# The Fourier step along the sequence, folded by a second symmetry (s and 384-s), with another order of the tokens

## The chip, the cores and the metric

The kernel runs on one core of a Trainium2 chip. The metric is the device time of one execution in microseconds (us). The profile comes from one execution taken by the hardware profiler; its span goes from the first to the last instruction. The engines are PE (TensorE, products), PEld (its weight loads), DVE (VectorE), ACT (ScalarE), POOL (GpSimd) and SP (SyncE, which issues most DMAs). SBUF is the on-chip memory of 128 partitions, PSUM the memory into which TensorE writes.

## The reference

There are two stages. First block-sparse attention for 4 batches and 8 heads, with 768 tokens and 64 features a head; then a Fourier mixing layer on the joined heads (768 x 512 per batch).

```python
scores = scale * np.matmul(q, k.transpose(0, 1, 3, 2))
scores = np.where(mask, scores, -1000000000.0)
attn = np.exp(scores - np.max(scores, axis=-1, keepdims=True))
attn = attn / (np.sum(attn, axis=-1, keepdims=True) + 1e-09)
x = np.matmul(attn, v)          # then (B, H, S, D) -> (B, S, H*D)

X = np.fft.fft(x, axis=1)       # along the sequence, S = 768
X = np.fft.fft(X, axis=2)       # along the features, 512
u = x + np.real(X)
un = (u - mean(u)) / np.sqrt(var(u) + 1e-06)
out = u + np.maximum(un @ w_ch1, 0.0) @ w_ch2     # 512 -> 2048 -> 512
```

Everything is computed in fp32.

## The kernel before, in words

**Tiles and the order of tokens.** The 768 tokens of a batch lie in six tiles of 128 rows. Tiles 0 to 2 form half 0 (`xA`), tiles 3 to 5 half 1 (`xB`), and row p of tile t in half 1 holds token (768 - s) mod 768 where row p of tile t in half 0 holds token s, apart from the ends. The order within the tiles is written out in `_ORDER`. An entry is (tile, first row, runs, jump, n, first token, step): `runs` runs of n rows each, the tokens of a run `step` apart, the runs `jump` apart. `_rows` turns an entry into DMA access patterns: with a positive jump one DMA with the dimensions [runs, n, columns], otherwise one DMA per run with [n, columns]. It serves the loads of the sine and cosine tables (`table_s`) and the stores of the output (`store`). `_TURNED` and `_IN_ORDER` are the same order as copies on ScalarE that place the columns of q: `turn` for the first five pairs of heads, `in_order` for the other eleven.

**Attention.** A pair of heads is 12 units; two units form a slot. For a slot TensorE makes the scores (`s`, L573), in some slots adds the mask by a product (L583), ScalarE takes the exponential (L593, L601), VectorE multiplies by the mask in later slots (L603), TensorE makes the values (`o`, L647), and sums are added up on GpSimd or VectorE (L633, L628). The result of a pair is transposed into x by `place` (L670 on TensorE, L671 on ScalarE) or by DMAs (`place_blocks`, L686).

**The Fourier step.** `fourier` computes the real part of the two transforms by symmetries: fold_0 makes sa = xA + xB and sd = xA - xB (s against 768-s), fold_1 and fold_2 fold the features twice, and fold_e makes `e1`, tile 1 of sa with another sign in row 0. `along(g)` multiplies along the sequence: for g = 0 and 1 the cosine part (`cosine`: two products over all 385 columns for tiles 0 and 2, then 192 and 193 columns for e1 and tile 1), for g = 2 and 3 the sine part (three products of 384 columns, L855); at g = 2 the 32 leftover columns go to `side` (L849). `keep_cosine` evacuates with three copies. `across(m)` then multiplies along the features, `arrive` adds to x, `spread` and `whiten` normalise.

**The channel layers.** `quad` makes a block of the first layer with seven products (L1045) and `channels` the second layer for one x tile (L1101, added to x at L1104). For batches 0 to 2 `channels` calls `store` for each tile after the last block; the last batch uses `outputs` (L1164) with stores in halves of the columns.

**The order of work.** The program is written out in order by a planner. It keeps an estimate of each engine's time (`when`) and of free PSUM banks, and takes the mixer's steps (`apart`, each with estimated costs) between the products of attention (`slot`) and of the channel layers of an earlier batch (`late`) where they seem ready (`gap`). Steps behind the folds wait until at most six channel steps are left. x has two buffers for each half, so batch b takes the buffer of batch b-2: `until` runs channel steps until the stores of that half are issued, and the first `place` of the new batch, whose copy is on ScalarE, writes into it.

Of the kernel before, what the change touches and what calls it, by code (L numbers as in the profile page):

```python
# [11 lines left out]
FP32 = mybir.dt.float32  # L12
# [5 lines left out]
ALU = mybir.AluOpType  # L18
# [22 lines left out]
def _grid(ap, start, runs, jump, n, step):  # L41
# [21 lines left out]
_TURNED = (((0, 64, 192, -64, 64, 1), (256, 64, 256, -192, 64, 1), (129, 63, 385, -384, 63, 1),  # L63
            (128, 127, 0, 384, 1, 1), (641, -128, 383, 127, 63, -1), (512, 127, 320, 191, 1, 1)),
           ((384, 64, 191, 64, 64, -1), (704, -128, 64, 63, 63, -1), (640, 127, 0, 1, 1, 1)))

_IN_ORDER = ((0, 129, (256, 127, 2), (64, -128, 2), (1, 2, 64)),  # L70
# [32 lines left out]
def kernel(  # L103
# [19 lines left out]
    P = 128  # L123
# [22 lines left out]
    cs_sb = const.tile([P, T, KS], FP32, name="cs_sb")  # L146
    sn_sb = const.tile([P, T, KS - 1], FP32, name="sn_sb")
# [5 lines left out]
    alt = const.tile([96, QD + 1], FP32, name="alt")  # L153
# [11 lines left out]
                            op0=ALU.mult)  # L165
    mask = const.tile([P, C, S], U8, name="mask")
# [212 lines left out]
    def table_s(src, dst, t):  # L379
        raw = tr_p.tile([P, ND * HS], FP32, tag="tr", name="tab")  # L380

        def get():
            for p0, cnt, rows in _rows(src, t):
                nc.sync.dma_start(out=raw[p0:p0 + cnt, 0:KS], in_=rows)

        def put():
            to = 0
            for runs, jump, n, s0, step in ODD_EVEN if dst is cs_sb else AS_PLACED:
                nc.vector.tensor_copy(
                    out=dst[:, t, to:to + runs * n].rearrange("p (r n) -> p r n", r=runs),  # L390
                    in_=_grid(raw, s0, runs, jump, n, step))
                to += runs * n
        return get, put

    AS_PLACED = [o[2:] for o in _ORDER if o[0] < T]
    ODD_EVEN = [AS_PLACED[i] for i in (0,)] + [(1, 0, 63, 259, 2), AS_PLACED[3], AS_PLACED[1],
                                               (1, 0, 63, 2, 2), AS_PLACED[4], (1, 0, 1, 384, 1)]

    def table_d(src, dst):
# [7 lines left out]
        def put():  # L407
            if dst is cd_sb:
                nc.vector.memset(alt, 0.0)
                for to, frm in ((dst, raw), *((alt[g:g + 1, :], row) for g in (0, 32, 64))):  # L410
                    nc.vector.tensor_copy(out=to[:, 0:QD + 1], in_=frm[:, 0:KD:2])
                nc.vector.tensor_copy(out=dst[:, QD + 1:KD], in_=raw[:, 1:KD:2])
            else:
# [6 lines left out]
                   for t in range(T)]  # L420
# [70 lines left out]
    def turn(n, a, half):  # L491
# [19 lines left out]
        else:  # L511
            for i, (to, to_jump, frm, jump, cnt, step) in enumerate(_TURNED[half]):
                on, copy = (("DVE", nc.vector.tensor_copy) if n == 0 and half == 1
                            else ("ACT", nc.scalar.copy))
                copy(out=_grid(dst, to, 2, to_jump, cnt, 1),
                     in_=_grid(tp, frm, 2, jump, cnt, step))
                end = busy(on, 0.27 if cnt > 1 else 0.18, done)
# [250 lines left out]
    def fourier(b, xA, xB, uns):  # L768
# [17 lines left out]
        def fold_e():  # L786

            sa, _, e1 = st["f"]
            b1 = xB[:, 1, :]
# [3 lines left out]
                                           in1=sa[:, 1, 0:M + 1], op0=ALU.mult, op1=ALU.add)  # L793

        def fold_2(i):
# [3 lines left out]
            if i != 1:  # L799
# [9 lines left out]
        folds = [lambda: fold_0(0), lambda: fold_0(1), lambda: fold_1(0), fold_e,  # L809
                 lambda: fold_1(1), lambda: fold_2(0), lambda: fold_2(2), lambda: fold_2(1)]  # L810

        parts = slice(DM - QD, DM), slice(0, QD)

        def along(g):
# [7 lines left out]
            odd = S // 4  # L822

            def cosine(ps, rows, cols):
                mm = nc.tensor.matmul
                for t in (0, 2):
                    mm(ps[rows, 0:KS], sa[:, t, cols], cs_sb[:, t, :], start=(t == 0), stop=False)  # L827
                mm(ps[rows, 0:odd], e1[:, cols], cs_sb[:, 1, 0:odd], start=False, stop=False)
                mm(ps[rows, odd:KS], sa[:, 1, cols], cs_sb[:, 1, odd:KS], start=False, stop=True)

            def keep_cosine(dst, ps):
                nc.scalar.copy(out=dst, in_=ps[:, 0:KS])

                nc.scalar.copy(out=_grid(dst, P + 1, 2, 63, 63, 1),
                               in_=_grid(ps, P, 2, 65, 63, 1))
                nc.scalar.copy(out=_run(dst, P, 2, P - 1), in_=_run(ps, P + 64, 2, -1))

            if g < 2:
                cosine(ps, slice(0, P), parts[g])
                keep_cosine(st["zc"][:, g, :], ps)  # L840
                return
            if g == 2:
                side, at = ps_t.tile([P, 512], FP32, tag="t", name="side"), bank("t")
                for i, (lhs, t, cols) in enumerate(((sa[:, 0, :], 0, slice(0, KS)),
                                                    (sa[:, 2, :], 2, slice(0, KS)),
                                                    (e1, 1, slice(0, odd)),
# [772 lines left out]
```

## Time and profile before

| | us |
|---|---|
| time, median of 3 runs | 1061.93 (1061.48 to 1063.14) |
| span of the profiled execution | 1059.7 |
| mean of one 128x385 record (L827) / 128x192 (L828) / 128x384 (L855) | 0.493 / 0.324 / 0.497 |
| all records of L827, L828, L829, L855, L849 together, busy | 11.9 + 3.9 + 3.9 + 17.3 + 5.5 |
| VectorE, scalar_tensor_tensor over 257 elements (L792), each | 0.488 |
| ScalarE, evacuations of the cosine part (L832, L834, L836), each | 0.481, 0.264, 0.162 |

A line of a group has the line of the kernel, the engine, the operation, output and inputs, shapes, the number of records, then busy time and mean of one, then the idle time ahead of them. A matmul's record reaches to its modelled end and overlaps the next one's, so the time that a product occupies TensorE is read from the distance of the starts. An fp32 product makes two records. In the DMA rows, the digit is the mean share of 16 DMA engines in tenths, and the row of GB/s is what they moved in each of 40 equal slices.

### The profile page before, as it was taken

How to read it: one execution, taken by the hardware profiler on the slowest of the kernel's cores; microseconds unless marked ns; L12 is line 12 of the kernel's file. 1: busy time of each engine (PE TensorE's matmuls, PEld its weight loads, DVE VectorE, ACT ScalarE, POOL GpSimd, SP SyncE). 2: the span in 40 equal slices, each digit the busy share in tenths (PEclk: the TensorE clock that was granted, in tenths of full speed). 3: DMA queues.
4: the chain of work that ended last, by engine and by line, in shares of the span. 5: the costliest groups of instructions: out<-in, count | busy, mean ns of one | idle time of the engine just before them, and what ended most of it. 6: DMA issues, size and time to landing. Idle time of an engine off the chain costs nothing.

```text
span 1059.7 us, 12422 instructions
## 1 busy us (share of the span) xinstructions
PE 1036.7 (98%) x4390; PEld 535.8 (51%) x4390; DVE 654.7 (62%) x1218; ACT 374.3 (35%) x742; POOL 235.6 (22%) x262
## 2 busy tenths in 40 slices
PE   8999999999999999999999999999999999999996
PEld 4333345444455554444444555444445554578575
DVE  6898894667645445664668364765457455575663
ACT  6978855664030112342441302253220211210210
POOL 1000183537000002454553001256520001000000
PEclk9999999999999999999999999999999999999998
DMA  7757422220000002212220001221000001000001
GB/s 214 231 168 232 117 46 45 45 47 15 1 0 1 1 0 48 59 29 54 42 54 2 1 0 30 60 38 28 11 11 6 1 0 32 29 0 1 1 20 43
DMA packets 120803, 46.65 MB, mean 44 GB/s; under 512 B 108176, under 2 KB 113822, under 8 KB 120734
## 3 DMA queue, kind: packets, MB, share of 16 engines
q1 hardware_dynamic: 119484, 45.06, 17.3%
q10 hardware_dynamic: 1218, 0.72, 0.3%
q8 instruction: 36, 0.59, 0.2%
q14 instruction: 33, 0.27, 0.1%
q0 software_dynamic: 32, 0.01, 0.0%
HBM read 37.11 MB, written 6.29 MB: 41 GB/s over the span
## 4 chain that ended last, share of the span: by engine, by line
PE 89%; DVE 4%; DMA 3%; ACT 2%; issue 1%; SPq 0%; POOL 0%; ACTq 0%; DVEq 0%
PE y L1101 23%; PE z L1045 15%; PE s L573 12%; PE o L647 10%; PE yp L1045 7%; PE yy L1164 7%; PE xp L1045 4%; PE zp L855 2%; DMA out_dram<-x 1%; PE s L583 1%; PE zp L827 1%; PE sp L714 1%; PE sp L728 1%; PE utp L970 1%; PE xt L670 1%
## 5 line engine op out<-in xcount | busy, mean ns | idle before, releaser
L633 POOL TENSOR_TENSOR acc<-acc,e 128x384 f32<-128x384 f32 x158 | 159.3, 1042 | 94.1 <-DVE e L603 75.1
L573 PE MATMUL s<-qT,kT 64*128 64x384 f32 x768 | 154.0, 516 | 7.7 <-ACT e L593 4.3
L647 PE MATMUL o<-e,vr 128*64 128x384 f32 x768 | 141.8, 497 | 0.0
L1101 PE MATMUL y<-w_sb,hB 128*128 128x512 f32 x288 | 128.2, 596 | 1.0 <-DVE x L1104 1.0
L1101 PE MATMUL y<-w_sb,hA 128*128 128x512 f32 x288 | 128.4, 595 | 0.0
L603 DVE TENSOR_TENSOR e<-s,mask 128x768 f32<-128x768 f32 x92 | 83.8, 951 | 57.6 <-ACT s L601 47.8
L1104 DVE TENSOR_TENSOR x<-y,x 128x512 f32<-128x512 f32 x72 | 49.7, 690 | 110.9 <-PE y L1101 110.8
L573 PEld LDWEIGHTS s<-qT,kT 64*128 64x128 f32 x768 | 64.2, 186 | 85.8 <-issue 22.1
L601 ACT ACTIVATE s<-s 128x768 f32<-128x768 f32 x92 | 69.9, 792 | 87.5 <-PE s L573 87.0
L1045 PE MATMUL z<-unT,t 128*128 128x384 f32 x256 | 93.1, 486 | 1.2 <-DVE hA L1050 1.2
L633 POOL TENSOR_TENSOR acc<-e 128x384 f32<-128x384 f32 x42 | 47.1, 1142 | 211.6 <-ACT e L593 126.7
L1050 DVE TENSOR_TENSOR hA<-z,hA 128x384 f32<-128x384 f32 x64 | 35.7, 557 | 87.5 <-PE z L1045 87.5
L593 ACT ACTIVATE e<-s 128x768 f32<-128x768 f32 x100 | 76.1, 815 | 36.2 <-PE s L583 31.2
L1101 PEld LDWEIGHTS y<-w_sb,hB 128*128 128x128 f32 x288 | 53.4, 190 | 67.7 <-issue 65.0
L918 POOL TENSOR_SCALAR st<-st 128x1 f32<-128x1 f32 x24 | 8.6, 358 | 346.9 <-DVE st L917 346.8
L1101 PEld LDWEIGHTS y<-w_sb,hA 128*128 128x128 f32 x288 | 53.3, 190 | 62.8 <-issue 59.7
L647 PEld LDWEIGHTS o<-e,vr 128*64 128x64 f32 x768 | 47.9, 136 | 70.3 <-issue 67.9
L1054 ACT ACTIVATE hA<-hA 128x384 f32<-128x384 f32 x64 | 33.5, 523 | 120.3 <-DVE hA L1050 119.9
L1045 PEld LDWEIGHTS z<-unT,t 128*128 128x128 f32 x256 | 48.5, 190 | 35.5 <-DVE hA L1050 2.1
L1054 ACT ACTIVATE hB<-hB 128x384 f32<-128x384 f32 x64 | 33.5, 523 | 86.5 <-DVE hB L1050 84.2
L1065 ACT COPY hA<-xp 128x384 f32<-128x384 f32 x32 | 15.3, 478 | 97.9 <-PE xp L1045 97.9
L1045 PE MATMUL xp<-unT,w_sb 128*128 128x384 f32 x128 | 47.2, 492 | 0.0
(202 smaller groups left out, 1428.7 us busy)
## 6 DMA issues: line engine op xcount, KB each, us to landing
wraw<-in_moe_w_ch_dram SPq DMA_DIRECT2D x32, 512.0 KB
vr<-in_v_dram SPq DMA_DIRECT2D x30, 192.0 KB
qb<-in_q_dram SPq DMA_DIRECT2D x44, 96.0 KB
kb<-in_k_dram SPq DMA_DIRECT2D x44, 96.0 KB
x<-oT SPq DMA_DIRECT2D x192, 12.0 KB
out_dram<-x SPq DMA_DIRECT2D x15, 128.0 KB
out_dram<-x SPq DMA_DIRECT2D x7, 256.0 KB
qr<-in_q_dram SPq DMA_DIRECT2D x24, 64.0 KB
```

Source lines behind the costliest of these rows:

```text
L573: nc.tensor.matmul(s[:, i, 0:HS], kT[rows, c * P:(c + 1) * P], qT[rows, queries], start=True, stop=u not in by_pe)
L593: nc.scalar.activation(out=e, in_=s[:, :, 0:HS], func=ACT.Exp, scale=scale)
L601: nc.scalar.activation(out=s[:, :, 0:HS], in_=s[:, :, 0:HS], func=ACT.Exp, scale=scale)
L603: nc.vector.tensor_tensor(out=e, in0=s[:, :, 0:HS], in1=m.broadcast_to([P, 2, HS]), op=ALU.mult)
L633: nc.gpsimd.tensor_add(out=acc[:, i, :], in0=start[:, i, :], in1=e[:, i, :])
L647: nc.tensor.matmul(o[D * i:D * i + D, :], vt[:, i, c, :], e[:, i, :], start=(c == 0), stop=(c == C - 1))
L1045: nc.tensor.matmul(to, a[:, k, :], c[:, k, :], start=(k == 0), stop=(k == ND // 2 - 1))
L1050: tt(out=to, in0=ps, in1=a, op=ALU.add)
L1054: nc.scalar.activation(out=h, in_=h, func=ACT.Relu)
L1101: nc.tensor.matmul(y, hs[0, half][:, l, m * P:(m + 1) * P], w2_sb[:, 4 * r + l, :], start=(l == 0), stop=(l == 3))
L1104: nc.vector.tensor_tensor(out=x[:, m, :], in0=y, in1=x[:, m, :], op=ALU.add)
L1164: nc.tensor.matmul(ps, a[:, k, :], c[k // 2][:, k % 2, :] if isinstance(c, list) else c[:, k, :], start=(k == 0), stop=(k == 3))
```

## The change

The token order now pairs s with 384-s as well: tiles 0 and 1 of half 0 hold the tokens 0 to 255, tile 2 the tokens 384-s for tile 0 (with 256, 257 at its ends), and half 1 the mirrored ones. With this a second fold (`fold_s`, six VectorE operations per batch) makes from tiles 0 and 2 one tile for the odd and one for the even frequencies. Each frequency column then needs two products instead of three, and the table tiles for t = 2 are gone. The columns of the tables are placed in the order odd, even (`FREQUENCIES`), the evacuation (`keep`) restores an order with whole tiles, the frequency 384 and token 0 now lie in m = 0 instead of m = 1, and the planner's lists and estimated costs follow. `_TURNED` and `_IN_ORDER` become lists of copies with up to three dimensions, and the lists of two runs in `_ORDER` have a jump of 1.

```diff
-_ORDER = ((0, 0, 2, -128, 64, 129, 2),
-          (1, 0, 1, 0, 1, 0, 1), (1, 1, 2, -257, 63, 259, 2), (1, 127, 1, 0, 1, 257, 1),
-          (2, 0, 2, -128, 64, 256, 2),
-          (3, 0, 2, 128, 64, 639, -2),
-          (4, 0, 1, 0, 1, 384, 1), (4, 1, 2, 257, 63, 509, -2), (4, 127, 1, 0, 1, 511, 1),
-          (5, 0, 2, 128, 64, 512, -2))
+_ORDER = ((0, 0, 2, 1, 64, 0, 2), (1, 0, 2, 1, 64, 128, 2),
+          (2, 0, 1, 0, 1, 256, 1), (2, 1, 2, 1, 63, 382, -2), (2, 127, 1, 0, 1, 257, 1),
+          (3, 0, 1, 0, 1, 384, 1), (3, 1, 2, 1, 63, 766, -2), (3, 127, 1, 0, 1, 641, 1),
+          (4, 0, 1, 0, 1, 640, 1), (4, 1, 2, 1, 63, 638, -2), (4, 127, 1, 0, 1, 513, 1),
+          (5, 0, 1, 0, 1, 512, 1), (5, 1, 1, 0, 63, 386, 2), (5, 64, 1, 0, 64, 385, 2))
...
-    cs_sb = const.tile([P, T, KS], FP32, name="cs_sb")
-    sn_sb = const.tile([P, T, KS - 1], FP32, name="sn_sb")
+    cs_sb = const.tile([P, 2, KS], FP32, name="cs_sb")
+    sn_sb = const.tile([P, 2, KS - 1], FP32, name="sn_sb")
...
+    first_row = ident[:, 0:1]
+    not_first = const.tile([P, 2], FP32, name="not_first")
...
+        def fold_s(i):
+
+            def plus(out, tile, by, to):
+                nc.vector.scalar_tensor_tensor(out=out[:, 0:M + 1], in0=tile[:, 0:M + 1], scalar=by,
+                                               in1=to[:, 0:M + 1], op0=ALU.mult, op1=ALU.add)
+
+            sa, sd, e1 = st["f"]
+            if i == 0:
+                plus(e1, sa[:, 2, :], not_first[:, 1:2], e1)
+                plus(sa[:, 0, :], sa[:, 2, :], not_first[:, 0:1], sa[:, 0, :])
+                plus(sa[:, 1, :], sa[:, 2, :], first_row, sa[:, 1, :])
+                plus(sa[:, 2, :], sa[:, 2, :], flip, sa[:, 1, :])
+            else:
+                plus(sd[:, 0, :], sd[:, 0, :], not_first[:, 0:1], sd[:, 2, :])
+                plus(sd[:, 2, :], sd[:, 2, :], -2.0, sd[:, 0, :])
...
-            def cosine(ps, rows, cols):
-                mm = nc.tensor.matmul
-                for t in (0, 2):
-                    mm(ps[rows, 0:KS], sa[:, t, cols], cs_sb[:, t, :], start=(t == 0), stop=False)
-                mm(ps[rows, 0:odd], e1[:, cols], cs_sb[:, 1, 0:odd], start=False, stop=False)
-                mm(ps[rows, odd:KS], sa[:, 1, cols], cs_sb[:, 1, odd:KS], start=False, stop=True)
...
+            def keep(dst, ps, n):
+                nc.scalar.copy(out=_at(dst, 64, [(-64, 2), (P, T), (1, 64)]),
+                               in_=_at(ps, 0, [(ODD, 2), (64, T), (1, 64)]))
+                if n == KS:
+                    nc.scalar.copy(out=dst[:, n - 1:n], in_=ps[:, n - 1:n])
+
+            def product(to, table, *terms):
+                ps, ks = to
+                for t, lhs in enumerate(terms):
+                    nc.tensor.matmul(ps, lhs, table[:, t, ks], start=(t == 0), stop=(t == 1))
...
-                cosine(ps, slice(0, P), parts[g])
-                keep_cosine(st["zc"][:, g, :], ps)
+                cols = parts[g]
+                product(odd(ps, slice(0, P)), cs_sb, e1[:, cols], sa[:, 2, cols])
+                product(even(ps, slice(0, P), ODD + 1), cs_sb, sa[:, 0, cols], sa[:, 1, cols])
+                keep(st["zc"][:, g, :], ps, KS)
...
-            for t in range(T):
-                nc.tensor.matmul(ps[:, 0:KS - 1], sd[:, t, parts[g - 2]], sn_sb[:, t, :],
-                                 start=(t == 0), stop=(t == T - 1))
-            nc.scalar.copy(out=zs[:, g - 2, 0:KS - 1], in_=ps[:, 0:KS - 1])
+            cols = parts[g - 2]
+            product(odd(ps, slice(0, P)), sn_sb, sd[:, 0, cols], sd[:, 1, cols])
+            product(even(ps, slice(0, P)), sn_sb, sd[:, 2, cols], sd[:, 1, cols])
+            keep(zs[:, g - 2, :], ps, KS - 1)
...
-                 d(1.0, fold_1, 1), d(1.2, fold_2, 0), d(0.6, fold_2, 2), d(1.3, fold_2, 1)]
-        first += [("mt" if g == 2 else "m", lambda g=g: along(g), 2.1, (1.0 if g < 2 else 0.5), 0.0)
+                 d(1.0, fold_1, 1), d(1.8, fold_s, 0), d(1.2, fold_2, 0), d(0.6, fold_2, 2),
+                 d(0.9, fold_s, 1), d(1.3, fold_2, 1)]
+        first += [("mt" if g == 2 else "m", lambda g=g: along(g), (2.1 if g == 2 else 1.4), 0.5, 0.0)
```

More of the change, by code (lines that the diff above doesn't have):

```diff
@@ L419 @@
     table_steps = [(table_s, (src, dst, t)) for src, dst in ((cos_s, cs_sb), (sin_s, sn_sb))
-                   for t in range(T)]
+                   for t in range(2)]
     table_steps += [(table_d, (cos_d, cd_sb)), (table_d, (sin_d, sd_sb))]
@@ L896, in arrive @@
             x = (xA, xB)[half][:, m, :]
-            if m == 1 and half == 1:
+            if m == 0 and half == 1:
                 row = st["zs"][0:1, 0, :]
```

102 lines of the change are left out of this document (49 added, 53 removed), and 10 rows, old and new, of tables (_IN_ORDER, _TURNED).

## The prediction

> **What bounds the kernel now.** I read the page first: span, busy times, the slices and the chain of waits.
>
> ```profile
> span 1059.7 us, 12422 instructions
> PE 1036.7 (98%) x4390; PEld 535.8 (51%) x4390; DVE 654.7 (62%) x1218; ACT 374.3 (35%) x742; POOL 235.6 (22%) x262
> PE   8999999999999999999999999999999999999996
> ...
> PE 89%; DVE 4%; DMA 3%; ACT 2%; issue 1%; SPq 0%; POOL 0%; ACTq 0%; DVEq 0%
> ```
>
> TensorE is the bound nearly everywhere: busy 98%, 89% of the chain. A product taken away shortens the run if nothing else makes TensorE stand. The three medians lie 2.2 us above this span (1061.93 against 1059.70); I build the sum on the span and add 2.2 at the end.
>
> Next, the timeline of TensorE where batch 2 is transformed; start, length, engine, line, tile. Ends are modelled, so I take differences of starts.
>
> ```profile
> 583.64 1.46 PE L827 MATMUL zp<-cs_sb,sa 128*128 128x385 f32 x4
> 584.94 0.49 PE L828 MATMUL zp<-cs_sb,e 128*128 128x192 f32 x2
> 585.26 0.49 PE L829 MATMUL zp<-cs_sb,sa 128*128 128x193 f32 x2
> 585.59 1.45 PE L1045 MATMUL yp<-t,w_sb 128*128 128x384 f32 x4
> ...
> 597.48 2.20 PE L855 MATMUL zp<-sn_sb,sd 128*128 128x384 f32 x6
> 599.52 1.45 PE L1045 MATMUL yp<-t,w_sb 128*128 128x384 f32 x4
> ```
>
> Each fp32 product is two records. One over 385 columns takes (584.94-583.64)/2 = 0.65 us, one over 192 takes 0.32, so the time goes with the columns, down to half the width.
>
> The third view is the stores of x, by their DMA traffic: first the three x tiles of half 0 of batch 2, then the three of half 1.
>
> ```profile
> GB/s 0 0 0 0 0 0 116 212 191 225 130 0 0 0 0 0 0 7 0 150 184 130 198 178 27 0 0 0 0 0 0 0 198 212 219 205 41 0 0 0
> ...
> GB/s 0 0 25 16 49 20 29 45 20 57 49 49 49 57 49 49 49 41 37 37 45 49 53 49 53 49 49 53 49 53 49 53 49 70 49 53 33 0 0 0
> q1 hardware_dynamic: 392, 0.79, 11.2%
> ```
>
> The first row covers 885 to 897 us (0.3 us a slice): each tile is gone in some 1.5 us at about 200 GB/s. The second covers 898 to 918 (0.5 us a slice): the same 0.79 MB needs 17.5 us at 49 GB/s, and 11.2% of 16 engines over 20 us is 36 engine-us, so two engines work. The two halves differ in how `_rows` describes the rows. Tiles 0 to 2 are issued as single runs of 63 or 64 rows (their jump is negative, so the runs are split). Tiles 3 to 5 have a positive jump: one DMA whose outermost dimension is the two runs. Two runs, two engines.
>
> Last, what a late store costs: the stage in which batch 2's x takes over the buffer of batch 0.
>
> ```profile
> 408.64 0.49 PE L670 MATMUL xt<-ident,oT 128*128 128x128 f32 x3
> ...
> 412.25 0.48 ACT L671 COPY x<-xt 128x384 f32<-128x384 f32 x1 [2.82 <-PE o L647]
> 412.63 1.51 ACT L601 ACTIVATE s<-s 128x768 f32<-128x768 f32 x2
> 413.47 1.82 DVE L603 TENSOR_TENSOR e<-s,mask 128x768 f32<-128x768 f32 x2 [4.37 <-ACT s L601]
> ...
> 414.48 1.78 PE L573 MATMUL s<-qT,kT 64*128 64x384 f32 x8 [1.12 <-DVE e L603]
> ```
>
> The copy into x (L671) has its input by 409.1 but starts at 412.25. The `o` named is not an input; what it must wait for is the last of the three stores of that buffer, issued at 409.6. Behind it on ScalarE stand the exps, behind them VectorE's masks, behind them TensorE's scores, which stood 1.12 us. So this chain already reaches TensorE.
>
> **The change, part by part.**
>
> *Products along the sequence.* Per batch, two cosine groups go from two 385-column products plus 192 and 193 (1.95 us, 583.64 to 585.59) to four of 192 or 193 (4 x 0.325 = 1.30): 2 x 0.65 = 1.30 less. Two sine groups go from three of 384 (2.04 us, the second 1.93) to four of 192 (1.30): 1.26 less after a switch of some 0.1. The side products, which run beside each other in groups of 32 columns, take about 0.7 us either way. 2.56 x 4 batches = **-10.2 us** (bounds -10.9 to -9.6). This step stands on rows of the very same shapes.
>
> *VectorE and ScalarE.* fold_s adds six SCALAR_TENSOR_TENSOR over 257 elements per batch; L792, the same form, takes 0.49 us with 0.40 from start to start: 24 x 0.40 = 9.6 us in all. In batches 0 to 2 they lie under products (TensorE is busy 12.00 of 12 us from 300 to 312). In batch 3 the folds end at 814.6 and the first product along the sequence follows at 817.6; 2.4 us more uses that slack up, and a missed gap moves it to 822. Its last whitening ends at 872 and the first transposes that are held for the last six channel steps come at 878.4, so 4.5 us still fits. If it didn't, it would cost up to that much. I take **+0.5** (0 to +4.5). The evacuations lose two small copies for each cosine group. The reordering of q on ScalarE goes from six copies (2 x 0.43, 2 x 0.31, 2 x 0.20) to seven, 0.2 us more in 11 pairs on an engine that is 35% busy: nothing.
>
> *Start and tables.* Two tables fewer are loaded and copied (18 small copies of 0.14 to 0.22 us, two waits of SP's queue for a free buffer). Against it, four of the remaining loads get two runs, hence two engines: 128 rows of 1.5 KB, some 4 us each at 49 GB/s, in the stretch in which weight loads once kept ScalarE waiting 3.3 us. The mask's query spread gets 4 more casts of 0.11 us, twice, and VectorE two setup instructions; off_q is ready at 8.0 us and first used at 9.0. I take **+0.5** (-2 to +2).
>
> *Stores of x.* This is a part that the words of the change do not name. All two-run entries of the new `_ORDER` have jump +1: tiles 0 and 1 become one two-run DMA each, tile 2 two single rows and a two-run DMA, tiles 3 and 4 likewise; only tile 5 is single runs (1, 63 and 64 rows). So the slow form moves from half 1 to the whole of half 0 and two tiles of half 1: 1.30 MB per batch on two engines where it was 0.78.
>
> Where half 0 is reused, the price can be worked out. For batch 2 the stores start at 401.38, 405.25 and 409.13; first bytes come 1.05 us after an issue (885.75 to 886.8). 0.782 MB at 49 GB/s is 16.0 us, so the last byte leaves at 418.4; at the 42 GB/s that half 1 had here (421.8 to 440.3) it is 420.9. I take 419.0, because VectorE and GpSimd stand still meanwhile, plus 0.4 to the copy (440.2 to 440.65 in half 1): 419.4 instead of 412.25. Nothing else is queued on TensorE ahead of those scores: **+7.2** (+5 to +9). For batch 3 the stores start at 651.78: last byte 652.8 + 16.6 = 669.4, copy at 669.9, first masks 0.4 + 0.85 us later, scores 1.0 after that, 672.1 instead of 668.17: **+4.0** (0, if the planner puts another channel step ahead of the copy, to +6). Half 1 gains: its copy waited 1.86 us for the last store at 440.65 and TensorE stood 0.74; with tile 5 spread that goes: **-0.7** (-0.7 to 0).
>
> *The end.* Before, the last packet (1057.1) belongs to tile 5 of half 1, on two engines. Now tile 4 and tile 1 (0.25 MB each) are followed on the same two engines by the two halves of tile 2's rows (0.13 MB, 2.6 us each), the second issued after 1051.4: from 1039 with 252 KB at the slow 14 to 24 packets per us seen there to 1046.4, 256 KB to 1051.7, then 2.9, 1.0 for tile 5's share and 2.9, so 1058.5: **+1.4** (-1 to +2.2).
>
> The Trainium skill (DMA: Bandwidth & Descriptors, section Why a DMA increments its semaphore by 16 and not by 1) says that a DMA runs on the largest number of engines up to 16 that divides the slowest dimension of both access patterns, whatever its steps; for the new entries that is two engines again, which makes the first rival below less likely than the rows alone do.
>
> Sum: -10.2 + 0.5 + 0.5 + 7.2 + 4.0 - 0.7 + 1.4 = +2.7. 1059.7 + 2.7 + 2.2 = **1064.6 us**: slower, though TensorE has less to do.
>
> **The rivals.**
> 1. The stores don't stay on two engines: every two-run store in the trace has a row step of -2, the new tiles 0 and 1 have +2 and a jump of one row. If they spread, all waits stay as they are: 1061.9 - 10.2 + 0.8 = 1052.5, faster. For it: no two-run row with a positive step exists. Against: single runs of either step spread. 0.12.
> 2. The two waits are half covered, as the planner lays a channel step (3.4 us) ahead of each copy, as it did in batch 3 (659.55 to 663.1): 1064.6 - 2 x 2.1 = 1060.4. Against: for batch 2 there was none. 0.20.
> 3. VectorE's folds miss gaps in the last batch (+4.5) or the table loads delay the weights (+2): about 1069. 0.13.
> 4. The forecast, 1064.6, with a range of its own of 1060.5 to 1068. 0.55.
>
> **Chances.** A measurement here tells some 0.2% (2.1 us) from no change: 1059.8 to 1064.1 is the same. The forecast puts 0.43 above and 0.12 within; rival 1 all below; rival 2 0.06 below and 0.14 within; rival 3 all above. That is 0.18 faster, 0.26 same, 0.56 slower. The range, 1056 to 1069.5, leaves rival 1 and a tail of rival 3 out.
>
> **What would show it.** Records of 192 columns at 0.32 us a product and no 384 ones in `zp`; six more instructions of the form of L792 per batch; DMA at 49 GB/s for some 16 us after half 0's last stores; the copy into x some 7 us later after its transposes than before for batch 2, and the scores behind it; for half 1 no wait. Wrong if half 0's stores run at 200 GB/s, if TensorE's busy time falls by much less than 10 us, or if stalls appear at the folds.

## The result and the profile after

The changed kernel takes **1099.54 us** (median of 4 runs, 1098.12 to 1099.61) against 1062.08 us before (4 runs, 1061.48 to 1063.14): a ratio of **1.0349, 95% interval 1.0335 to 1.0364**, 37.5 us slower. The forecast was slower by 2.7. The direction was right, the size was not: 1099.5 lies far outside the range of 1056 to 1069.5.

The page of the changed kernel: the span, busy time of each engine, TensorE's busy tenths, the granted clock in tenths, and the head of the chain of waits, by engine.

```profile
span 1097.8 us, 12462 instructions
PE 1043.4 (95%) x4414; PEld 542.8 (49%) x4414; DVE 666.8 (61%) x1231; ACT 366.9 (33%) x736; POOL 230.7 (21%) x258
...
PE   8969999998999998999999998978999999999995
...
PEclk9989999999999998999999999999999999999998
...
PE 81%; DVE 5%; SPq 4%; DMA 4%; ACT 3%; issue 1%; POOL 0%; DVEq 0%; ACTq 0%; POOLq 0%
```

TensorE stands in places where it did not: at slices 3, 10, 16, 25 and above all 27 and 28 of 40. Outside its busy time there were 23.0 us before (1059.7 - 1036.7); now there are 54.4 (1097.8 - 1043.4). And its busy time, which should have fallen by 10, rose by 6.7: part of it runs at a lower granted clock, as the row PEclk shows at two of these places (the kernel's mean is 0.984, before 0.995).

The saving itself is there. Timeline of TensorE in batch 2, the first cosine group along the sequence (start, length, line, tile):

```profile
608.54 0.49 PE L854 MATMUL zp<-cs_sb,e 128*128 128x192 f32 x2
608.87 1.14 PE L854 MATMUL zp<-cs_sb,sa 128*128 128x192 f32 x6
609.85 1.45 PE L1064 MATMUL yp<-t,w_sb 128*128 128x384 f32 x4
```

From 608.54 to 609.85 is 1.31 us for four products; the forecast was 1.30, before it was 1.95.

The first place that the forecast had not seen, SP's queue from 59 us (L387 loads a table, L389 the one row that replaces row 0 of the sine table, L261 is q, L454 the weights; an `x6` is six issues in a row):

```profile
59.09 0.55 SPq L387 DMA_DIRECT2D tab<-in_sin_s_dram  x1
65.42 0.27 SPq L389 DMA_DIRECT2D tab<-in_sin_s_dram  x1
65.81 3.85 SPq L261 DMA_DIRECT2D qr<-in_q_dram  x6
69.71 1.55 SPq L454 DMA_DIRECT2D wraw<-in_moe_w_ch_dram  x3
```

The row lands in the same partition as row 0 of the load ahead of it, so its issue waits until that load has landed: SP does nothing from 59.64 to 65.42. The view of SP's waits (what waited for what: us in total, times, longest) says the same:

```profile
SPq L389 <- DMA tab<-in_sin_s_dram: 5.7, 1, 5.7
```

Behind it stand six loads of q and the weights. What that does on TensorE (in brackets the idle time before, and what ended it):

```profile
67.47 0.85 PE L717 MATMUL sp<-e,pick 128*32 128x384 f32 x8
76.84 2.93 PE L576 MATMUL s<-qT,kT 64*128 64x384 f32 x8 [8.52 <-ACT e L596]
```

ScalarE waited 9.41 us for the weights' chunk (its L463 at 74.89), the exps stand behind that, and TensorE stood 8.52 us. The scores after it take 2.93 us where eight records of them otherwise take 1.56. The kernel before has a shorter stop at this place, and the scores behind it are slow too; its granted clock is 0.57 from 70 to 74 us:

```profile
70.01 2.46 PE L573 MATMUL s<-qT,kT 64*128 64x384 f32 x8 [2.40 <-ACT e L593]
```

The second place was forecast, the copy of batch 2's x into the buffer of batch 0. ScalarE, and TensorE beside it:

```profile
422.68 0.59 ACT L990 COPY unT<-utp 128x512 f32<-128x512 f32 x1 [3.90 <-PE utp L989]
429.25 0.48 ACT L674 COPY x<-xt 128x384 f32<-128x384 f32 x1 [5.98 <-DMA out_dram<-x]
```

```profile
422.48 0.49 PE L673 MATMUL xt<-ident,oT 128*128 128x128 f32 x3
...
431.47 2.93 PE L576 MATMUL s<-qT,kT 64*128 64x384 f32 x8 [4.28 <-DVE e L606]
```

Its input is there by 423.0, the copy waits for the store of the old x until 429.25; again the scores behind the stop take 2.93 us. The same happens for batch 3: the copy starts at 684.50, the scores at 686.73 after 4.46 us of idle time.

The third place is the largest: the attention of the last batch. Work in windows of 20 us (busy time and instructions of PE, PEld, DVE, ACT, POOL, then the granted clock, DMA share, GB/s), after and then before:

```profile
710.00:730.00 20.00, 16.19 (x92) 6.23 (x92) 12.75 (x15) 10.94 (x22) 17.31 (x19) 1.00 0.23 37
730.00:750.00 20.00, 15.47 (x80) 5.60 (x80) 13.07 (x15) 8.53 (x12) 14.20 (x15) 0.91 0.16 35
750.00:770.00 20.00, 16.23 (x78) 5.77 (x75) 11.36 (x16) 5.09 (x7) 16.34 (x17) 0.91 0.12 18
```

```profile
710.00:730.00 20.00, 20.00 (x91) 8.11 (x88) 11.31 (x15) 8.92 (x17) 11.58 (x12) 1.00 0.20 41
730.00:750.00 20.00, 20.00 (x81) 7.95 (x79) 9.34 (x12) 5.43 (x8) 7.69 (x8) 1.00 0.07 11
```

Before, TensorE was full there: channel products of batch 2 ran between the scores. After, there are none in this stretch; batch 2's first `y<-w_sb,hA` (record 192 of that tile) starts at 788.28 instead of 716.24 (before, then after):

```profile
716.24 1.98 PE L1101 MATMUL y<-w_sb,hA 128*128 128x512 f32 x4
...
788.28 4.03 PE L1120 MATMUL y<-w_sb,hA 128*128 128x512 f32 x9
```

Attention alone leaves TensorE waiting 12.1 us in these three windows: 5.8 for VectorE's masks (L606), 5.1 for its output transposes (L658), the rest for sums. The transposes themselves wait there, 9.8 us in all, for the DMA that carries an earlier block out of the same buffer (`x<-oT`).

At the end, TensorE's last product ends at 1086.04 and the span 11.7 us later; before it was 8.8 us.

### The profile page after: what moved, and what is told of

Its sections match the earlier page's. It is cut to its first block, busy times and chain, and to the rows that moved or that the text cites. A ratio compares the mean times of both kernels' runs of the same rounds, so it can differ in the third digit from the quotient of the medians.

```text
span 1097.8 us, 12462 instructions
## 1 busy us (share of the span) xinstructions
PE 1043.4 (95%) x4414; PEld 542.8 (49%) x4414; DVE 666.8 (61%) x1231; ACT 366.9 (33%) x736; POOL 230.7 (21%) x258
## 4 chain that ended last, share of the span: by engine, by line
PE 81%; DVE 5%; SPq 4%; DMA 4%; ACT 3%; issue 1%; POOL 0%; DVEq 0%; ACTq 0%; POOLq 0%
PE y L1120 22%; PE z L1064 15%; PE s L576 10%; PE o L650 8%; PE yp L1064 7%; PE yy L1183 6%; PE xp L1064 4%; SPq L689 3%; PE zp L854 2%; DMA out_dram<-x 2%; PE s L586 1%; PE sp L717 1%; DVE t L1026 1%; DMA x<-oT 1%; DMA wraw<-in_moe_w_ch_dram 1%
## 5 line engine op out<-in xcount | busy, mean ns | idle before, releaser
L576 PE MATMUL s<-qT,kT 64*128 64x384 f32 x768 | 159.3, 530 | 30.6 <-DVE e L606 18.7
L636 POOL TENSOR_TENSOR acc<-acc,e 128x384 f32<-128x384 f32 x152 | 154.0, 1047 | 74.3 <-DVE e L606 47.9
L606 DVE TENSOR_TENSOR e<-s,mask 128x768 f32<-128x768 f32 x88 | 80.2, 949 | 58.2 <-ACT s L604 52.4
L604 ACT ACTIVATE s<-s 128x768 f32<-128x768 f32 x88 | 67.4, 793 | 87.6 <-PE s L576 87.2
L596 ACT ACTIVATE e<-s 128x768 f32<-128x768 f32 x104 | 79.3, 813 | 48.6 <-PE s L586 36.0
L1064 PE MATMUL z<-t,w_sb 128*128 128x384 f32 x128 | 46.6, 487 | 0.5 <-DVE t L1026 0.5
```

What stands on the lines that cost most here:

```text
L576: nc.tensor.matmul(s[:, i, 0:HS], kT[rows, c * P:(c + 1) * P], qT[rows, queries], start=True, stop=u not in by_pe)
L596: nc.scalar.activation(out=e, in_=s[:, :, 0:HS], func=ACT.Exp, scale=scale)
L604: nc.scalar.activation(out=s[:, :, 0:HS], in_=s[:, :, 0:HS], func=ACT.Exp, scale=scale)
L606: nc.vector.tensor_tensor(out=e, in0=s[:, :, 0:HS], in1=m.broadcast_to([P, 2, HS]), op=ALU.mult)
L636: nc.gpsimd.tensor_add(out=acc[:, i, :], in0=start[:, i, :], in1=e[:, i, :])
L1064: nc.tensor.matmul(to, a[:, k, :], c[:, k, :], start=(k == 0), stop=(k == ND // 2 - 1))
```

## The experiments

Thirteen kernels, each beside runs of the kernel before on the same chip; differences are between the medians of a run and of the kernel before measured beside it. Where a run is set against the changed or a mended kernel, that kernel's own median is used. The first theory: three causes, namely stores of x on two DMA engines, the queue behind the sine row, and the planner's order in the last attention. Rivals: that VectorE's added work is what is late, and that the waits only show it.

**Stores spread.** In `store` every run is one DMA with ascending rows.

```diff
+        if by_run:
+            s0, jump, step = ((s0, jump, step) if step > 0 else
+                              (s0 + step * (n - 1), jump, -step))
-        if jump > 0:
+        if jump > 0 and not by_run:
```

> The changed kernel with every store of x issued as one DMA per run of rows, each ascending (so that it spreads over more than two engines); the rows of tiles 2, 3 and 4 land in the output in the reverse order within a run. Nothing else is changed: same steps in the same order. Theory: two-engine stores cause the two late copies into x (7.7 us for batch 2, some 4.5 us for batch 3), the low granted clock behind each (about 2 us of work lost), and 2 to 3 us at the end. So 12 to 19 us less: 1081 to 1088 us, no PE idle time of 5 us at 425 us and 4 us at 685. Rival: the copies are late because the mixer's steps come late, and the stores are covered: 3 us less at most, 1096 or more.

Measured 1084.36 us (1.0203, 1.0186 to 1.022): 15.2 less than the changed kernel, as the theory has it. Lined up with the changed kernel's profile, 7.2 us go at batch 2's copy, 6.1 at batch 3's and 3.0 at the end; 1.7 are lost in between, behind a stop at 257 us that both kernels have (more on it below).

**The sine row aside.**

```diff
-                nc.sync.dma_start(out=raw[0:1, 0:KS], in_=src[P:P + 1, :])
+                nc.sync.dma_start(out=raw[0:1, KS:2 * KS], in_=src[P:P + 1, :])
...
+                    if dst is sn_sb and t == 0:
+                        nc.vector.tensor_copy(out=dst[0:1, t, to:to + n],
+                                              in_=_run(raw[0:1, :], KS + s0, n, step))
```

> The changed kernel with the one-row load that replaces row 0 of the sine table sent to a free part of the tile, and copied into place by VectorE with the table (five one-row copies more). The table loads stay on two engines. Theory: the row's load waited on SP's queue for the table load to land, 5.8 us, and the loads of q and the weights stood behind it; TensorE's 8.5 us idle at 68 to 77 us shrinks to the 2.4 us it was before, and the low clock behind it with it: 6 to 10 us less, 1090 to 1094 us. Rival: the weights are late because table loads on two engines hold up the queue's transfers, whoever waits: 2 us less at most, 1097.5 or more.

1094.87 us (1.0317, 1.03 to 1.0335), 4.7 less; 5.6 in the profiles from slot 16 on, 6.1 at the end of batch 2's channel layers. SP's queue now:

```profile
59.59 0.55 SPq L387 DMA_DIRECT2D tab<-in_sin_s_dram  x1
60.18 0.49 SPq L389 DMA_DIRECT2D tab<-in_sin_s_dram  x1
60.78 3.85 SPq L261 DMA_DIRECT2D qr<-in_q_dram  x6
66.31 1.30 SPq L457 DMA_DIRECT2D wraw<-in_moe_w_ch_dram  x3
```

The row no longer waits, and the weights go out 3.4 us sooner; TensorE's stop shrinks from 8.52 to 3.35 us (2.40 before). So most of it was the wait, and by these stops the loads on two engines cost about a microsecond by themselves. The size is below the theory's 6 to 10.

**fold_s without steps of its own.**

```diff
-                 d(1.0, fold_1, 1), d(1.8, fold_s, 0), d(1.2, fold_2, 0), d(0.6, fold_2, 2),
-                 d(0.9, fold_s, 1), d(1.3, fold_2, 1)]
+                 d(1.0, lambda: (fold_1(1), fold_s(0))), d(1.2, fold_2, 0), d(0.6, fold_2, 2),
+                 d(1.3, lambda: (fold_s(1), fold_2(1)))]
```

> The changed kernel with the two fold_s steps not planned as steps of their own: each runs inside its neighbour (fold_1 and fold_2), at the neighbour's planned cost. The same instructions are issued; only the planner's order differs: batch 2's channel layers are released during slot 79, before the channel steps of batch 1 run out, instead of in slot 95. Theory: that order is what stretches the last attention phase, where TensorE had no channel products beside the scores: 18 to 26 us less, 1074 to 1081 us, and y<-w_sb,hA number 192 starts some 70 us sooner. Rival: VectorE's own added work is what is late, and the order only shows it: 4 us less at most, 1095 or more.

1091.62 us (1.0284, 1.0267 to 1.0301), 7.9 less: between the theory's 18 to 26 and the rival's 4. Lined up with the changed kernel, the last attention and what follows it gain 11.3 us (from +2.6 ahead of it to -8.7 behind), but batch 0's mixer loses some 5 at slot 36, of which 1.3 to 2.6 stay. The order counts, for the better there and for the worse in batch 0, where four folds now stand behind one another and TensorE stops 2.37 us (165.29 to 167.65). What the folds cost by themselves this run can't show, as the changed kernel has the same ones.

**All three mended.** Ascending runs (stores and tables) one DMA each, the two-run tile 2 stored first of its half, the row aside, the steps merged. What is new in it:

```diff
-        if jump > 0:
+        if jump > 0 and not (by_run and step > 0):
...
-                     for half in range(2) for m in range(T)]
+                     for half in range(2) for m in ((2, 0, 1), (0, 1, 2))[half]]
```

> The changed kernel with all of it mended and a correct output: ascending runs (tables and stores) one DMA per run, the slow tile 2 of half 0 stored first of its half instead of last, the sine row loaded to a free part, and fold_s inside its neighbours. Theory: the three causes explain all of it, and what is left is the saving of 10 us on the products against 1062 us, with 1 to 4 us of store wait: 1052 to 1057 us. Rival: there is a fourth cost of the change that stays, VectorE's 24 added instructions or the new forms of copies, some 10 us: 1062 or more.

1067.43 us (1.0054, 1.0037 to 1.0071): the rival. It takes back 32.1 of the 37.5 us, and yet it stands 5.7 above before where the products alone should have put it 10.2 below: some 16 us of other costs stayed. The next runs looked for these from the other side, by adding one thing at a time to the kernel before.

**Only the products saved.**

```diff
-                for t in (0, 2):
+                for t in (0,):
                     mm(ps[rows, 0:KS], sa[:, t, cols], cs_sb[:, t, :], start=(t == 0), stop=False)
...
-            for t in range(T):
+            for t in range(2):
```

> The kernel before, with one product left out of each group along the sequence (the 385-column product of tile 2 in each of two cosine groups, tile 2 of the three in each of two sine groups), so that TensorE has as much to do there as in the changed kernel; the transform lacks tile 2's part. The planner's estimates and its order stay those of before. Theory A, the prediction's term: TensorE is the bound in all four batches, 10.2 us less, 1051 to 1053 us. Theory B: only batches 1 and 2, where channel products fill TensorE on both sides, give their 2.6 us; in batch 0 attention alone and in batch 3 VectorE's folds set the pace: 5 to 7 us less, 1055 to 1057 us.

1051.91 us (0.9897, 0.988 to 0.9913), 10.5 less. Theory A, in all four batches: lined up with the kernel before, 2.4 to 2.6 us go in each.

**Only the folds added.** Four instructions of fold_s's form in fold_1's step, two in fold_2's.

```diff
+        def fold_s(i):
+            s = st["f"][i]
+            for t in range(2 if i else 4):
+                nc.vector.scalar_tensor_tensor(out=s[:, t % T, M + 1:DM], in0=s[:, 2, 1:M],
+                                               scalar=flip, in1=s[:, 0, 1:M],
+                                               op0=ALU.mult, op1=ALU.add)
```

> The kernel before, with six more instructions on VectorE per batch, of fold_s's form over 255 columns, four behind fold_1 and two ahead of fold_2, written to columns that are dead there; unknown to the planner, so its order is that of before. Theory A, the prediction's term: they lie under products, 0 to 1 us more, 1061.5 to 1063. Theory B: in batch 0, where GpSimd works beside, one takes 1.22 us instead of 0.48, and the attention's sums wait behind them on VectorE; in batch 3 the add behind the channel product waits: 2 to 3 us each, 4 to 6 us more in all, 1066 to 1068.

1068.25 us (1.0051, 1.0034 to 1.0068), 5.8 more: theory B. Its profile is that of its slowest execution (1071.60), and 4.3 us of the lateness in it lie ahead of 105 us, where no fold has run. Behind that, batch 0's mixer adds 4.0 us, batch 2's 0.5, batch 3's 1.6. VectorE in batch 0, and GpSimd at the same time:

```profile
159.03 4.64 DVE L799 SCALAR_TENSOR_TENSOR sa<-sa,flip 128x255 f32<-128x255 f32 x4
163.59 0.54 DVE L696 COPY sums<-sp 128x384 f32<-128x384 f32 x1
...
165.64 0.87 DVE L799 SCALAR_TENSOR_TENSOR sd<-sd,flip 128x255 f32<-128x255 f32 x2
```

```profile
158.19 2.91 POOL L633 TENSOR_TENSOR acc<-e 128x384 f32<-128x384 f32 x2 [0.49 <-PE sp L728]
161.07 2.31 POOL L633 TENSOR_TENSOR acc<-acc,e 128x384 f32<-128x384 f32 x2
```

Beside GpSimd's adds (158.2 to 163.4) one takes 1.16 us; two microseconds later, with GpSimd at rest, 0.43. The copy of the sums stands behind the four, and TensorE's next transposes wait for it:

```profile
164.19 0.55 PE L670 MATMUL xt<-ident,oT 128*128 128x128 f32 x3 [2.35 <-DVE sums L696]
```

**Only two empty steps.** The kernel before, with two steps in the planner's list whose function is empty: they issue nothing.

```diff
+        def fold_s(i):
+            pass
...
-                 d(1.0, fold_1, 1), d(1.2, fold_2, 0), d(0.6, fold_2, 2), d(1.3, fold_2, 1)]
+                 d(1.0, fold_1, 1), d(1.8, fold_s, 0), d(1.2, fold_2, 0), d(0.6, fold_2, 2),
+                 d(0.9, fold_s, 1), d(1.3, fold_2, 1)]
```

> The kernel before, with two empty steps in the planner's list per batch, of fold_s's estimated cost, that issue no instruction. All instructions are those of before; their order becomes that of the changed kernel: batch 2's channel layers are released in slot 95 instead of 79. Theory A: the order alone costs 8 to 16 us (12 of them in the last attention phase, worked out from the run with the steps inside their neighbours, where the shift fell from +3 to -9 us there): 1070 to 1078. Theory B: the order is harmless and what costs is VectorE's work in it: within 3 us of before, 1059 to 1065.

1082.26 us (1.0189, 1.0172 to 1.0206): **19.8 us more from two steps that do nothing**, above even theory A's range. It is not quite the order alone, though. The planner also chooses the engine of each mask and each sum by its estimates, and in its new order it made four masks by products on TensorE that VectorE made before (groups before, then in this run):

```profile
L603 DVE TENSOR_TENSOR e<-s,mask 128x768 f32<-128x768 f32 x92 | 83.8, 951 | 57.6 <-ACT s L601 47.8
...
L603 DVE TENSOR_TENSOR e<-s,mask 128x768 f32<-128x768 f32 x88 | 80.0, 949 | 47.7 <-ACT s L601 41.7
```

Three additions of sums also went from GpSimd to VectorE. The changed kernel has 88 masks on VectorE as well. The eight mask records more are some 0.7 us on TensorE by their starts (four in 0.33 us), so I take the order to be the main part; the two were not tried apart. In its profile the shift is +2.5 up to slot 76 and +18.6 from the end of batch 2's channel layers on, so 16 of it lie in the last attention:

```profile
690.00:710.00 20.00, 15.49 (x88) 5.67 (x84) 12.78 (x15) 11.98 (x22) 15.99 (x18) 1.00 0.29 46
710.00:730.00 20.00, 14.37 (x76) 5.09 (x74) 11.53 (x14) 8.04 (x12) 12.56 (x14) 0.91 0.16 36
730.00:750.00 20.00, 16.42 (x89) 6.28 (x89) 14.88 (x19) 6.68 (x9) 18.85 (x19) 1.00 0.12 18
```

TensorE stands 13.7 us in these three windows (60 less 46.3), again for masks (6.4) and output transposes (6.2).

**The mended kernel in before's order.** The planner's estimate of a group along the sequence back from 1.4 to 2.1 us.

```diff
-        first += [("mt" if g == 2 else "m", lambda g=g: along(g), (2.1 if g == 2 else 1.4), 0.5, 0.0)
+        first += [("mt" if g == 2 else "m", lambda g=g: along(g), 2.1, (1.0 if g < 2 else 0.5), 0.0)
```

> The mended kernel (one DMA per ascending run, tile 2 first, the sine row aside, fold_s inside its neighbours) with the planner's estimate of the products along the sequence put back to before's 2.1 us, so that its order is that of the kernel before, also around slot 48 to 52. Theory: TensorE's idle 4.6 us at 245 to 260 us in the mended kernel comes from the shorter estimate, which put the last steps of batch 0's mixer ahead of the masks: 3 to 6 us less than its 1067.4, 1061 to 1064.5. Rival: the idle time comes with the folds and moves elsewhere: 1066 or more.

1062.61 us (0.9999, 0.9989 to 1.0008), 4.8 less than the mended kernel (1067.43): the theory, and level with before. The mended kernel's stop of 3.33 us ahead of the scores at 252.21 is gone; with it VectorE makes 92 masks again. So the shorter estimate, which is part of the change, had a price as well. Products less folds should have given 4.7 us under it, so something of that size was still hidden. It was in the products across the features, where each batch lost about 1.3 us. Their timeline in this kernel, batch 2:

```profile
624.10 0.39 PE L887 MATMUL pq<-cd_sb,zc 128*128 128x129 f32 x2
624.42 0.49 PE L888 MATMUL pq<-alt,zs 64*128 64x129 f32 x2
624.84 0.49 PE L889 MATMUL pq<-cd_sb,zc 128*128 128x128 f32 x2
625.25 0.38 PE L887 MATMUL end<-cd_sb,zc 128*1 128x129 f32 x2
```

The side products are kept in 64 rows instead of 96. The starts around the 64-row product lie 0.32, 0.42 and 0.41 us apart. (`alt` is the table for the side products.)

**96 rows again**, the third group filled with finite numbers that meet zeros in `alt`.

```diff
-    alt = const.tile([64, QD + 1], FP32, name="alt")
+    alt = const.tile([96, QD + 1], FP32, name="alt")
...
-                keep(zs[0:64, 2, :], side[0:64, :], KS)
+                keep(zs[0:96, 2, :], side[0:96, :], KS)
```

> The mended kernel with before's order, and the last part of the cosine product taken over 96 rows again instead of 64: the side products fill a third group of 32 rows with finite numbers, which the table meets with zeros. Theory: a product over 64 rows between products over 128 keeps them from following at 0.22 us: in the mended kernel the starts lie 0.32 and 0.42 us apart around it, 0.9 us more over three tiles and 0.3 at the last row, 1.2 us in each batch: 4 to 5 us less than its 1062.6, 1057.5 to 1059. Rival: the products wait there for VectorE or ScalarE anyway: less than 1.5 us less, 1061 or more.

```profile
620.85 0.39 PE L888 MATMUL pq<-cd_sb,zc 128*128 128x129 f32 x2
621.07 0.39 PE L889 MATMUL pq<-alt,zs 96*128 96x129 f32 x2
621.29 0.39 PE L890 MATMUL pq<-cd_sb,zc 128*128 128x128 f32 x2
621.61 0.38 PE L888 MATMUL end<-cd_sb,zc 128*1 128x129 f32 x2
```

With 96 rows the starts are 0.22 us apart. The weight loads of the second and third product show the difference; first with 64 rows, then with 96:

```profile
624.42 0.29 PEld L888 LDWEIGHTS pq<-alt,zs 64*128 64x128 f32 x2
624.83 0.30 PEld L889 LDWEIGHTS pq<-cd_sb,zc 128*128 128x128 f32 x2
...
620.96 0.30 PEld L889 LDWEIGHTS pq<-alt,zs 96*128 96x128 f32 x2
621.18 0.30 PEld L890 LDWEIGHTS pq<-cd_sb,zc 128*128 128x128 f32 x2
```

With 64 rows each load starts with its own product (624.42 and 624.84). With 96 it starts 0.11 us ahead (621.07 and 621.29), while the product before it still runs. **1057.65 us (0.996, 0.9946 to 0.9974)**, 4.4 us faster than before: with this the folded transform beats both kernels.

**Folds spread over five steps** (1, 2, 1, 1 and 1 instructions), on top of that.

```diff
+        parts_of = {3: (fold_e, (0,)), 4: (lambda: fold_1(1), (1,)), 5: (lambda: fold_2(0), (-2,)),
+                    6: (lambda: fold_2(2), (3,)), 7: (lambda: fold_2(1), (-4,))}
```

> As the run with 96 rows, and fold_s's six instructions spread over five neighbouring steps (1 behind fold_e, 2 behind fold_1, 1 ahead of fold_2, 1 behind it, 1 ahead of the last), at the planned cost of the neighbours alone. Theory: four in a row delay what stands behind them on VectorE (the sums in batch 0, the add of the channel layer in batch 3); spread, 1 to 3 us less than the run with 96 rows. Rival: VectorE has the same work to do ahead of the first product along the sequence, and nothing changes: within 0.7 us.

1057.5 us (0.9957, 0.9943 to 0.9971): no difference. The rival: VectorE has the same work ahead of the first product, however it is cut.

**64 rows in the kernel before**, the mirror: `alt` and its operand cut to 64 rows.

```diff
-            zc, zl = st["zc"], st["zs"][0:96, 2, :]
+            zc, zl = st["zc"], st["zs"][0:64, 2, :]
```

> The kernel before, with the last part of the cosine product cut from 96 rows to 64 (the third group's part is left out), nothing else. Theory: 1.2 us more in each batch where TensorE is the bound, 3.5 to 5 us in all: 1065.5 to 1067. Rival: a product over fewer rows costs no more: 1061.5 to 1062.7.

1067.57 us (1.0056, 1.0042 to 1.007), 5.5 more. The theory, slightly above its range.

**Two-run stores in the kernel before.**

```diff
+        if two and runs == 2 and jump < 0:
+            s0, jump = s0 + jump, -jump
```

> The kernel before, with the two runs of each tile of half 0 stored by one DMA whose outermost dimension is the two runs (the two runs land in each other's place in the output); tiles of half 1 are stored so already. Nothing else differs. Theory, the prediction's terms: the copy into x comes 7.2 us later for batch 2 and 4.0 for batch 3, and behind each stop the granted clock is low, 1 to 3 us more, so 12 to 17 us in all: 1074 to 1079. Rival: with before's order the waits are half covered, and the 15 us of the changed kernel came from its late steps: 3 to 8 us, 1065 to 1070.

1065.65 us (1.0033, 1.0023 to 1.0043), only 3.6 more. That looked like the rival, but the run did less than it was meant to: in tiles 0 and 2 the second run starts 128 rows on, just where 64 rows of step 2 end, so the two were issued as one even list of 128 rows and left in 2 us. Only tile 1 was slow. So it was repeated with the changed kernel's own transfers:

```diff
-            for p0, cnt, rows in _rows(out[b][:, cols], T * half + m):
+            for p0, cnt, rows in _rows(out[b][:, cols], T * half + m, _STORES):
```

Here `_STORES` is the changed kernel's `_ORDER`.

> The kernel before, storing x by the changed kernel's list of rows: tile for tile the same transfers as there, 1.30 MB per batch by two-run DMAs (the rows land in the wrong places of the output). Nothing else differs, the order is that of before. In the run before this one two of the three tiles had runs that follow each other evenly, and 128 rows left in 2 us over many engines; only one tile was slow. Theory: all three slow, the copy into x comes 7 us later for batch 2 and 4 for batch 3, 1 to 2 us of low clock behind each, and 1 to 3 us at the end: 12 to 17 us more, 1074 to 1079, as the 15 us that the changed kernel gave back with spread stores. Rival: a good part of those 15 us hung on the changed kernel's own order: 4 to 9 us more, 1066 to 1071.

1079.08 us (1.0159, 1.0145 to 1.0172), **17.1 more**. DMA from 400 to 424 us in 40 slices, ScalarE's copy, and two windows:

```profile
GB/s 0 0 0 0 0 20 27 34 27 38 31 48 48 55 48 55 48 55 48 55 48 123 123 55 48 55 48 79 167 55 48 63 182 33 27 150 30 0 0 0
```

```profile
420.76 0.48 ACT L678 COPY x<-xt 128x384 f32<-128x384 f32 x1 [10.71 <-DMA out_dram<-x]
```

```profile
415.00:420.00 5.00, 0.00 (x0) 0.00 (x0) 0.00 (x0) 0.00 (x0) 0.00 (x0) 0.65 0.34 86
420.00:425.00 5.00, 2.02 (x6) 1.13 (x8) 1.82 (x2) 3.41 (x7) 0.00 (x0) 0.50 0.17 27
```

The stores run for some 17 us, at 20 to 38 GB/s at first and then at 48 to 55 (the peaks are loads of k), the copy starts at 420.76 instead of 412.25, and the clock is at 0.50 when the scores come back.

## Why the prediction was right and wrong

| what | forecast, us | alone in the kernel before, or undone | measured, us |
| --- | --- | --- | --- |
| products along the sequence | -10.2 | only these | -10.5 |
| fold_s on VectorE | +0.5 | only these | +5.8 |
| start and tables | +0.5 | sine row aside | +4.7 |
| stores, both halves and the end | +11.9 | only these | +17.1 |
| the planner's order and choice of engines | none | empty steps | +19.8 |
| 64 rows instead of 96 | none | only these | +5.5 |

The measured column adds up to +42.4, the change cost +37.5: the causes share some 5 us, mainly stops that fall together in the last attention, I take it; that was not tried apart. The planner's shorter estimate, 4.8 us in the mended kernel, is not in the column and would come on top. Without the mendable ones, products and folds leave -4.7, and the mended kernel with 96 rows measured -4.4.

The step that failed worst is one that the sum doesn't have: the planner's two new steps and its new estimate were taken to change nothing, and the empty steps alone cost 19.8 us. Next to it, three terms were too small: the folds (5.8 us instead of 0.5), the start (4.7 instead of 0.5) and the stores (17.1 instead of 11.9). The direction was not luck: without the two causes that the forecast lacked, the measured terms still add up to +17.1. One of the prediction's own signs of being wrong came, as TensorE's busy time did not fall. Another, stalls at the folds, shows in the runs that issue four folds in a row.

- *Products along the sequence.* Right: 1.31 us a cosine group against 1.30, 10.5 us in all.
- *Stores of x.* The mechanism was right and its place exact. In the run with these stores alone the copy came 7.9 us later for batch 2 (forecast 7.2; 8.5 by the profile, which was 0.6 late already), and batch 3's scores 4.4 us later on top of that (forecast 4.0); half 1 gave 0.8 to 1.1 back (forecast 0.7); the end cost 2.3 (forecast 1.4). What the sum lacked is what a stop leaves behind: the first products after it run at half the granted clock, 1.6 us lost after the first stop and 2.2 after the second. The term should have had this added. The granted clock is 0.50 behind the stop of 9.0 us, and 0.55 in the changed kernel's window behind 4.3 us. The Trainium skill (TensorE: Matmul & The Clock Gate, section What's actually happening) says that the array falls to half rate after about one idle window of 3.4 us; these two stops agree. Shorter stops went both ways here: behind 2.40 us in the kernel before the clock was 0.57 from 70 to 74 us; behind the same 3.34 us ahead of batch 0's channel layers the next four records of `xp` took 2.93 us in the run with spread stores and 1.56 in the changed kernel.
- *VectorE and ScalarE.* "In batches 0 to 2 they lie under products" failed for batch 0, and so did "24 x 0.40": the view quoted for the cover, 300 to 312 us, is batch 1's stage, with channel products. Batch 0's mixer runs beside attention alone, while GpSimd adds, and there one of these instructions takes 1.16 us. The same could have been read in the profile before, where L790 takes 1.08 us in batch 0 and 0.41 in batch 3. The Trainium skill (GPSIMD Engine Reference, section 1. Specifications) names contention between GpSimd and VectorE instructions with two SBUF inputs; these have two, and the trace agrees. In the changed kernel itself five of batch 0's six folds take 1.11 to 1.22 us, and all of the other batches' 0.43 to 0.49. The 5.8 us are for four folds in a row inside fold_1's step, as in the mended kernels; in the changed kernel, where fold_s has steps of its own, TensorE has no stop of more than 0.9 us beside batch 0's folds, so what they cost there alone is open. In batch 3 the doubt about 4.5 us was well placed: 1.6 were lost.
- *Start and tables.* The term had the two-engine load ("some 4 us each") and the weights behind it, but not the one-row load: its issue, which writes where a load is still in flight, waited 5.7 us for that load, and the six loads of q and the weights were behind it on the same queue. The step that failed is that an added DMA was counted by its transfer and not by its wait.
- *What was left out.* Two more entries in a list that a planner spends gap by gap. They cost 2.7 us in its estimates; but the last three groups of batch 2's transposes (`utp`) then come behind the last channel product of batch 1 (at 679.5, 685.7 and 745.0 us with the empty steps, against one at 678.0 before), and batch 2's first channel block moves from slot 79 to slot 95 (678.5 to 752.0 us; 769.8 in the changed kernel). That VectorE's masks leave no gap for these steps is my reading and was not tried. Rival 3 asked only whether gaps are missed in the last batch, at 4.5 us. Also left out: "The side products ... take about 0.7 us either way" looked at the products and not at who reads their result, in 64 rows instead of 96.
- *Rivals.* Stores that spread and waits half covered are both ruled out by the run with these stores alone. Against the first, the prediction had "single runs of either step spread"; the stores and table loads of the kernel before have no descending single run of more than one row, so nothing in the trace stood behind the other step. Rival 3 had two of the right places, the folds and the weights, at less than they cost.

## What to carry to other kernels

A planner's list is part of the program: adding an entry, even an empty one, can move everything behind it and change which engine does the work. So the order and the number of instructions on each engine have to be compared with those before; two empty entries cost 19.8 us here. Count an added DMA by what its issue waits for and by what stands behind it on its queue. Count a stop of TensorE by its length and by the half clock behind it: 1.6 and 2.2 us here, after stops of 9.0 and 4.4. A duration is taken from the stage in which the instruction will run, with the engines that are busy there.

## What the runs showed of the hardware

- A product over 64 rows between products over 128 slows them: starts 0.32, 0.42 and 0.41 us apart instead of 0.22, with weight loads that start no sooner than their products, while 96 rows keep the pace. With three such products and a last row in each of four batches that is 5.5 us in the kernel before.
- Two runs of rows become one DMA over many engines if the second continues the first's step: 128 rows of 2 KB left in 2 us. With a jump that does not continue it, they went at 48 to 55 GB/s, as on two engines.
- VectorE's two-input instructions of 255 columns take 1.16 us beside GpSimd's adds and 0.43 without them.
- Behind the stops of TensorE of 8.52, 4.28 and 4.46 us in the changed kernel, and of 9.01 and 4.36 us in the last run, the granted clock is 0.50 while the next scores run (2.93 us instead of 1.56). A stop of 3.34 us was followed by the low clock in the run with spread stores and not in the changed kernel.
